# Filler stages beside lone tile stages, more gap matmuls, and longer planned landings in a planned delta-rule and MLP kernel

## The chip, the core and the metric

The kernel runs on one core of a Trainium2 chip. The metric is the device time of one execution in microseconds (us). The kernel before was timed three times: 564.54, 565.8 and 561.43 us, median 564.54. One further execution was profiled.

## What is computed

The reference is a gated delta rule (attention with a state that is corrected at every token) and a gated MLP on its output.

```python
# q, k, v: (4 batches, 8 heads, 768 tokens, 48); beta: (4, 8, 768)
k_n = k / (norm(k) + 1e-6)
for t in range(768):                       # S: (4, 8, 48, 48), from zero
    y[t] = q[t] @ S
    S = S + beta[t] * outer(k_n[t], v[t] - k_n[t] @ S)
x = y as (4, 768, 384)                     # heads side by side
h = relu(x @ w_in)                         # 384 -> 1024
u, v = h[..., :512], h[..., 512:]
v_n = (v - mean(v)) / sqrt(var(v) + 1e-6)
v_s = w_spatial @ v_n + b_spatial          # over the 768 tokens
out = (u * v_s) @ w_out                    # 512 -> 384
```

## The kernel before

**The delta rule, in chunks of 64 tokens.** Four batches of twelve chunks make 48 steps, all eight heads of a batch in one step. Four steps make a group, so there are 12 groups. For a group, K·Kᵀ (stage kk) is masked and scaled on VectorE (DVE) into `ta`. It goes to DRAM and back in another layout (`ad<-ta` L621, `la<-ad` L631, queued by SyncE, SP), and 30 dependent pairs of DVE operations (`prod` L647, `pw` L654) solve the triangular system in small blocks. The result goes through DRAM again (`wd`, then back into `ta`). Then come six stages for each step, each of them 8 or 16 small matmuls (64 x 48 and the like) on TensorE (PE) into one of four banks `pt` of PSUM: e and f finish the inverse (copied by ScalarE, ACT, L725 and L737), a makes the correction from the state (`pt<-st,kv`, then DVE `kv` L756), b applies the inverse (`pt<-kv,ta`, then DVE `us` L772), c makes the next state (`pt<-us,kv`, then DVE `st` L800), qk and d make the output (`pt<-aq,us` and `pt<-kv,st`; ACT copies it into `xs`, L845). All stage matmuls are recorded at one line, L415, of a helper. The chain from step to step is a, `kv`, b, `us`, c, `st`. Stage b of step s sets `line.cur` to s, from which due times are counted.

**Tile stages in pairs.** A stage uses two of PE's four 64 x 64 quadrants: the two on the diagonal (kind "diag") or the other two (kind "anti"). Two stages of different kinds can be issued in turns, matmul by matmul, as a pair. If only one is ready, or no second bank is free, a stage goes alone.

**The MLP.** Four steps of outputs in `xs` make a block of 256 tokens. `convert` moves the last heads to other partitions through DRAM (`xd<-xs` L869, `xs<-xd` L872), ACT rounds the block to `xh` (L888), and the rest goes to `xl` (L892). With every operand split into a high and a low part, the MLP is three matmuls for each product: `mlp_v` (L923), `mlp_u` (L989), the spatial product `mlp_g` (L1021, L1024), the output `mlp_o` (L1076). These use the whole array (kind "full"), the banks `pm`, and later `pw`, which the triangular solve uses first. The weights are loaded and split at L434 to L464. The norm of k runs ahead by groups (`knn` L537, a square root `nr` L541, DVE `t` L546 to L550).

**What sets the order.** The program is written out by a planner (class `Line`) that keeps a virtual clock for each of PE, DVE, ACT, GpSimd (POOL) and SP. Every job is a generator that yields `Op(eng, occ, lat, dep, due, kind, make)`: the engine, how long it is planned to hold the engine, how long until its result is there, when it can begin, and when it is due. `step` (L117) takes the operation that can begin earliest, and among those that begin nearly together the one due first. So a planned duration decides in which order instructions stand in each engine's queue, and the chip then executes each queue strictly in that order. A DMA is an `Op` on SP, and its planned landing time (`dma(dep, due, lat)`) decides where the operations that read it stand in the other queues.

`tensor` (L154) plans PE. `area` (L135) sums planned work of the last 3.4 us. Under `LOW` (3600) the planner prefers MLP work; under `HOT` (3050) it plans at half speed (`slow`), since PE's clock is granted in full only behind enough work. `keep_warm` (L143) fills planned gaps: as long as a gap of over 0.12 us is left and the area is under `FILL`, `idle` puts a matmul on a tile of ones (128 x 256, L1256 and L1259) into a free bank, whose result nobody reads. Below these are called gap matmuls. With four banks `pt` in `st_s` (class `Slots`, a list of free banks with the planned times from which they are free), a pair needs two of them (`line.room`).

Of the kernel before, what the change touches and what calls it, by code (L numbers as in the profile page):

```python
# [42 lines left out]
HOT = 3050  # L43
FILL = 4000

# [31 lines left out]
class Line:  # L77
# [4 lines left out]
    def __init__(self, t0):  # L82
        self.t = dict.fromkeys(("PE", "DVE", "ACT", "POOL", "SP"), t0)
        self.done = {}
        self.jobs = []
        self.mode = "full"
        self.cur = 0
        self.hist = []
        self.idle = self.room = None

# [66 lines left out]
    def tensor(self, e0, near):  # L157
# [81 lines left out]
def delta_rule_gated_mlp(  # L239
# [124 lines left out]

# [3 lines left out]
    st_s = Slots([x[:, 0:256] for x in banks])  # L368
    line.room = st_s.ready
    ob_s = Slots([sb(f"ob{i}", DM) for i in range(1)])  # L370
# [46 lines left out]
    def tiles_op(kind, dep, d, build, w):  # L417

        held = []

        def make():
            x = st_s.take()
            held.append(x)
            return build(psl(x[1], w))

        return Op("PE", 0, 1.3 * w, both(dep, st_s.ready), d, kind, make), held


    def load_w(buf, hi, lo, src, d):
        n = src.shape[1]  # L430
        st = buf[:, :n]
        if src.dtype == F32:
            t = yield dma(now, d, 6.0)
            nc.sync.dma_start(out=st, in_=src)  # L434
        else:
            raw = buf[:, 512 : 512 + 2 * n].bitcast(U32).rearrange("p (n two) -> p n two", two=2)
            t = yield dma(now, d, 6.0)
            nc.sync.dma_start(out=raw, in_=src.bitcast(U32).rearrange("p (n two) -> p n two", two=2))
# [71 lines left out]
    def norm(g):  # L510
# [68 lines left out]
    def kk(t):  # L579
# [3 lines left out]
        if t % n == 0:  # L583
# [40 lines left out]
    def load_la(g):  # L624
        d = due(4 * g - 7)
        src = ad_g[g].rearrange("j h n t -> (h n) j t")
        for blk in range(2):
            for par in range(2):
                l0, r0 = par * 64 + blk * 32, blk * 32
                t = yield dma(at(("ad", g), ("lanes", g - 2) if g > 2 else None), d, 4.2)  # L630
                nc.sync.dma_start(out=las[g % 2][l0 : l0 + 32], in_=src[:, r0 : r0 + 32, r0 : r0 + 32])  # L631
# [58 lines left out]
    def load_kv(s):  # L690
        t = yield dma(at(*((n, s - 3) for n in ("qk", "d", "a", "b", "c") if s >= 3)), due(s - 2.2), 4.5, 0.5)
        nc.sync.dma_start(out=kvs[s % 3], in_=kv_t[s])
# [171 lines left out]
    def convert(j, xs, t):  # L864
        x = xs[1].rearrange("p (u t) -> p u t", t=256)
        if j < NG2 - 2:
            xd = dram.tile([128, 256], F32, name="xd")
            t1 = yield dma(on(t), lately(0.3), 2.6)
            nc.sync.dma_start(out=xd[0:112], in_=x[0:112, 3])  # L869
            for h in range(2):  # L870
                t2 = yield dma(on(t1), lately(0.3), 2.6)
                nc.sync.dma_start(  # L872
# [307 lines left out]
    def widen(s, buf, pi):  # L1180
# [4 lines left out]
        nc.vector.transpose(out=tr.rearrange("p u t -> p (u t)"), in_=ta[:, s].rearrange("p u t -> p (u t)"))  # L1185
        t = yield Op("PE", 0.7, 1.0, both(on(t), pm_s.ready), d, "full")
        p = pm_s.take()
# [10 lines left out]
        nc.scalar.mul(out=pi[:, s], in_=pp, mul=hm)  # L1198
        t = yield Op("PE", 0.45, 0.75, on(t), d, "full")
        for u in range(NU):  # L1200
# [66 lines left out]

    line.idle = idle
    ET = mybir.EngineType
# [77 lines left out]
```

## Time and profile before

| what | value |
|---|---|
| three timed runs | 561.43, 564.54, 565.8 us |
| profiled execution, its own time | 563.41 us |
| its span in the trace | 561.7 us |
| mean granted clock of PE | 0.917 |
| busy: PE / weight loads / DVE / ACT / POOL | 500.4 / 451.8 / 355.0 / 218.9 / 142.7 us |
| DMA | 66.97 MB, 119 GB/s on the mean |
| first b stage, 28th, last | 62.8, 271.5, 483.1 us into the span |
| from the last b to the end | 78.6 us |

PE's row of busy time counts a matmul from its start to its modelled end. PEld is the load of the stationary operand, which runs beside the matmul before it. PEclk in the slices is the granted clock of PE in tenths of full speed (9 is 90% or more). In the windows view, each row is a stretch of the span, with busy time and number of instructions of each engine, the granted clock, the share of time in which DMA engines were busy, and their GB/s. In the timeline, a row is start, duration, engine, line, operation, tiles, and in brackets how long the engine was idle before it and what ended that. "issue" is time in which an engine waited for nothing that the profile shows.

### The profile page before, as it was taken

To read this page: it belongs to the slowest core of one execution; us is meant where nothing else is said; L and a number is where in the kernel's file an instruction comes from. 1 tells how busy PE (TensorE), PEld (TensorE's weight loads), DVE (VectorE), ACT (ScalarE), POOL (GpSimd) and SP (SyncE) were. 2 spreads that over 40 slices of the span, in tenths; PEclk is the share of its full clock that TensorE was granted. 3 is DMA by queue.
4 is the path that set the end of the run, shared out by engine and by line. 5 is a ranking of instruction groups with operands and counts; after the bars stand their busy time and mean duration, and the time that the engine had idled before them with its cause. 6 is when DMAs were issued, how large, how long until landed. Compare 5 with 4: busy or idle time off the path is not lost.

```text
span 561.7 us, 21394 instructions
## 1 busy us (share of the span) xinstructions
PE 500.4 (89%) x9040; PEld 451.8 (80%) x9040; DVE 355.0 (63%) x1434; ACT 218.9 (39%) x536; POOL 142.7 (25%) x212
## 2 busy tenths in 40 slices
PE   4936886987989989888989999999999999999997
PEld 4835775876777978788978789879987999898996
DVE  5899786976799978778958993258235341134210
ACT  3233433542636335423235645321256341137111
POOL 5534333653454341323213233311001000000000
PEclk8576695985989989989999999999999999999999
DMA  8687286768575738676865544461304010000001
GB/s 236 175 154 169 92 216 126 215 191 167 139 196 133 191 98 182 147 211 139 207 109 115 136 109 117 134 160 48 67 30 127 17 36 29 32 20 15 2 34 52
DMA packets 134252, 66.97 MB, mean 119 GB/s; under 512 B 105894, under 2 KB 123532, under 8 KB 134156
## 3 DMA queue, kind: packets, MB, share of 16 engines
q1 hardware_dynamic: 134156, 65.60, 47.9%
q8 instruction: 71, 1.16, 0.9%
q14 instruction: 25, 0.20, 0.1%
HBM read 50.11 MB, written 15.17 MB: 116 GB/s over the span
## 4 chain that ended last, share of the span: by engine, by line
PE 60%; DVE 16%; DMA 10%; ACT 4%; issue 4%; SPq 4%; POOL 1%; DVEq 0%; ACTq 0%
PE pt L415 20%; PE pm L1021 11%; PE pm L923 6%; PE pm L989 6%; PE pw L1021 5%; PE pm L1076 4%; PE pw L1076 3%; DVE pw L654 2%; DVE prod L647 2%; DMA knn<-in_k_nat 2%; PE pw L923 1%; DMA k<-in_kv_t 1%; DMA la<-ad 1%; SPq L631 1%; PE pw L989 1%
## 5 line engine op out<-in xcount | busy, mean ns | idle before, releaser
L654 DVE TENSOR_TENSOR pw<-pw,prod 128x96 f32<-128x96 f32 (+7 forms) x330 | 80.7, 250 | 4.6
L647 DVE TENSOR_TENSOR prod<-pw,la 128x126 f32<-128x126 f32 (+7 forms) x330 | 78.3, 242 | 7.9 <-ACT pw L641 2.9
L696 POOL TENSOR_TENSOR kv<-kv,cn 128x192 f32<-128x192 f32 x48 | 24.6, 513 | 142.8 <-DMA kv<-in_kv_t 122.8
L1021 PE MATMUL pm<-wsp_h,vh 128*128 128x256 f32 x204 | 60.2, 295 | 0.4 <-ACT vh L965 0.4
L415 PE MATMUL pt<-kv,st 48*64 48x64 f32 x768 | 55.5, 238 | 4.1 <-ACT ta L737 2.0
L1021 PE MATMUL pm<-wsp_h,vl 128*128 128x256 f32 x204 | 57.7, 283 | 0.2 <-DVE vl L969 0.2
L1021 PE MATMUL pm<-wsp_l,vh 128*128 128x256 f32 x204 | 57.7, 283 | 0.0
L415 PE MATMUL pt<-aq,us 64*64 64x64 f32 x768 | 53.4, 232 | 0.3 <-issue 0.3
L415 PEld LDWEIGHTS pt<-kv,st 48*64 48x64 f32 x768 | 44.0, 147 | 6.9 <-ACT ta L737 2.1
L415 PE MATMUL pt<-kv,ta 64*64 64x48 f32 x768 | 35.5, 231 | 10.4 <-DVE t L550 3.5
L415 PEld LDWEIGHTS pt<-aq,us 64*64 64x64 f32 x768 | 44.3, 148 | 0.4 <-issue 0.4
L415 PEld LDWEIGHTS pt<-kv,ta 64*64 64x64 f32 x768 | 29.7, 143 | 16.3 <-issue 5.8
L1038 DVE TENSOR_TENSOR tmp<-pm,ub 128x512 f32<-128x512 f32 x17 | 11.8, 691 | 48.8 <-PE pm L1024 48.8
L1057 ACT CAST gh<-tmp 128x512 fp32r<-128x512 f32 x24 | 14.8, 618 | 71.0 <-DVE tmp L1038 71.0
L415 PE MATMUL pt<-kv 48*64 48x64 f32 x768 | 35.7, 235 | 6.3 <-DVE t L546 4.7
L415 PE MATMUL pt<-k 48*64 48x64 f32 x640 | 29.4, 232 | 13.1 <-DVE nr L556 8.8
L1021 PEld LDWEIGHTS pm<-wsp_h,vh 128*128 128x128 f32 x204 | 38.8, 190 | 1.9 <-ACT vh L965 0.6
L415 PE MATMUL pt<-tn,ta 64*64 64x32 f32 x768 | 35.3, 234 | 5.2 <-DVE tn L711 3.8
L572 POOL TENSOR_TENSOR mc<-mpos,cn 128x256 f32<-128x256 f32 x46 | 28.6, 628 | 42.9 <-DVE ta L607 24.3
L1021 PEld LDWEIGHTS pm<-wsp_h,vl 128*128 128x128 f32 x204 | 39.0, 191 | 0.4 <-DVE vl L969 0.4
L1021 PEld LDWEIGHTS pm<-wsp_l,vh 128*128 128x128 f32 x204 | 39.0, 191 | 0.0
L415 PEld LDWEIGHTS pt<-tn,ta 64*64 64x64 f32 x768 | 30.7, 149 | 8.9 <-ACT wstage L442 3.8
(176 smaller groups left out, 1426.8 us busy)
## 6 DMA issues: line engine op xcount, KB each, us to landing
kv<-in_kv_t SPq DMA_DIRECT2D x48, 456.0 KB, 4.5
ad<-ta SPq DMA_DIRECT2D x24, 256.0 KB, 4.2
la<-ad SPq DMA_DIRECT2D x44, 128.0 KB, 4.4
out<-ob SPq DMA_DIRECT2D x24, 192.0 KB, 1.9
k<-in_kv_t SPq DMA_DIRECT2D x20, 224.0 KB, 3.9
knn<-in_k_nat SPq DMA_DIRECT2D x10, 384.0 KB, 5.6
wd<-w SPq DMA_DIRECT2D x22, 128.0 KB, 3.9
ta<-wd SPq DMA_DIRECT2D x44, 64.0 KB, 3.5
```

What stands on the lines that cost most here:

```text
L415: return lambda: nc.tensor.matmul(*a, **dict(dict(start=True, stop=True), **k))
L572: (nc.vector if t in (0, 2) else nc.gpsimd).tensor_tensor(out=mc, in0=mall, in1=cns[t // G][:, t % G, 1].unsqueeze(2).broadcast_to([128, N ...
L631: nc.sync.dma_start(out=las[g % 2][l0 : l0 + 32], in_=src[:, r0 : r0 + 32, r0 : r0 + 32])
L647: nc.vector.tensor_tensor(out=pr, in0=w[:, :n, j : j + 1].broadcast_to([128, n, m]), in1=la[:, j, j + 1 : 32].unsqueeze(1).broadcast_to([1 ...
L654: nc.vector.tensor_add(out=w[:, :n, j + 1 : 32], in0=w[:, :n, j + 1 : 32], in1=pr)
L696: nc.gpsimd.tensor_tensor(out=v, in0=v, in1=cns[s // G][:, s % G, 0].unsqueeze(2).broadcast_to([128, NU, HD]), op=ALU.mult)
L923: nc.tensor.matmul(p[1], a[:, kt, ts], w[:, kt, DH:], start=(n == 0), stop=(n == 3 * NK - 1))
L989: nc.tensor.matmul(pu[:, k], w[:, kt, d0 : d0 + 128], a[:, kt], start=(n == 0), stop=(n == 3 * NK - 1))
L1021: nc.tensor.matmul(pg[:, k], v[:, d0 : d0 + 128], w[:, si, ts], start=(n == 0), stop=False)
L1038: nc.vector.tensor_tensor(out=gt, in0=pg, in1=ut[:, hs], op=ALU.mult)
L1057: nc.scalar.copy(out=gh[:, hs], in_=gt)
L1076: nc.tensor.matmul(p[1][:, :DM], a[:, dd, ts], w[:, dd], start=(n == 0), stop=(n == 3 * ND - 1))
```

## The change

Four things, in the planner and in what it places:

1. **Filler stages.** A tile stage that finds no partner (`not f` in `tensor`) takes along a stage of the other kind that computes nothing of use: 8 or 16 matmuls of a constant (`mpos`) into a free bank, in turns with the real ones (`fake`). The condition `self.area(t) < FAKE` is always true with `FAKE = 99999`. A bank that got fillers is tagged with their kind, and until it is taken by a real stage of that kind it isn't given to another kind, nor to gap matmuls. `fake` gives nothing when no bank fits, and it opens a new one only if no bank has that kind's tag and two are free. `Slots` got the calls for this (`fit`, `ready_for`, `ready_both`), and a pair now needs one bank that fits "anti" and another that fits "diag".
2. **Gap matmuls up to a higher area.** `FILL` goes from 4000 to 7500; a gap matmul adds 256 for 0.107 us, so nearly every planned gap is filled.
3. **Longer planned landings.** Weights 6.0 to 9.0, `knn` 6.0 to 7.5, `k` 4.5 to 5.5, `la` 4.2 to 5.0, `kv` 4.5 to 6.0, `xd<-xs` 2.6 to 5.0, `xs<-xd` 2.6 to 3.8 us. The transfers are the same.
4. **Less weight for two small stages** of the first group in the history (150 for each us in place of 2300), so that the planner counts less area for them.

Lines behind the top of the kernel shift: L415 becomes L438, L845 and L888 become L868 and L911, L923 becomes L946, L989 becomes L1012, L1021 becomes L1044, L1076 becomes L1099, L1259 becomes L1282.

```diff
-FILL = 4000
+FILL = 7500
+FAKE = 99999
...
-        room = self.room(2)
+        room = self.room()
...
-            self.hist.append((self.t["PE"], op.occ * 2300))
+            self.hist.append((self.t["PE"], op.occ * (op.make or 2300)))
...
         lists = [o.make() for o, _ in picked]
         act_ = sum(o.lat * len(x) for (o, _), x in zip(picked, lists))
+        if not f and self.area(t) < FAKE:
+            more = self.fake("anti" if op.kind == "diag" else "diag", t, len(lists[0]))
+            if more:
+                lists.append(more)
+                act_ += 62 * len(more)
...
+            self.tag = {}
+
+        def fit(self, kind):
+            return sorted(f for f in self.free if self.tag.get(f[1], kind) == kind)
...
+        def ready_both(self):
+
+            a, d = self.fit("anti"), self.fit("diag")
+            t = [max(x[0], y[0]) for x in a for y in d if x[1] != y[1]]
+            return min(t) if t else None
 
-        def take(self):
-            f = min(self.free)
+        def take(self, kind=None):
+            f = min(self.free) if kind is None else self.fit(kind)[0]
             self.free.remove(f)
+            self.tag.pop(f[1], None)
             return f[1:]
...
-            x = st_s.take()
+            x = st_s.take(kind)
...
-            t = yield dma(now, d, 6.0)
+            t = yield dma(now, d, 9.0)
...
-            t = yield dma(at(("nr", g - 1), ("cn", g - 2)), d, 6.0, 0.5)
+            t = yield dma(at(("nr", g - 1), ("cn", g - 2)), d, 7.5, 0.5)
...
-            done["k", t] = yield dma(at(*busy), due(4 * g - 11), 4.0 if t < 2 * G else 4.5, 0.5)
+            done["k", t] = yield dma(at(*busy), due(4 * g - 11), 4.0 if t < 2 * G else 5.5, 0.5)
...
-                t = yield dma(at(("ad", g), ("lanes", g - 2) if g > 2 else None), d, 4.2)
+                t = yield dma(at(("ad", g), ("lanes", g - 2) if g > 2 else None), d, 5.0)
...
-            t1 = yield dma(on(t), lately(0.3), 2.6)
+            t1 = yield dma(on(t), lately(0.3), 5.0)
...
-                t2 = yield dma(on(t1), lately(0.3), 2.6)
+                t2 = yield dma(on(t1), lately(0.3), 3.8)
...
-        free = [f[2][:, 0:256] for k in (pm_s, st_s) for f in k.free if f[0] <= t]
+        free = [f[2][:, 0:256] for k in (pm_s, st_s) for f in k.free if f[0] <= t and f[1] not in k.tag]
...
+    def fake(kind, t, n):
+
+        fit = [f for f in st_s.fit(kind) if f[0] <= t]
+        own = [f for f in fit if f[1] in st_s.tag]
+        if not own and (kind in st_s.tag.values() or len(st_s.free) < 2):
+            return None
+        f = (own or fit or [None])[-1]
+        if f is None:
+            return None
+        st_s.tag[f[1]] = kind
+        p = psl(f[2], HD)
+        r = [
+            mm(p[rows_t(h) if kind == "diag" else rows_s(h), u], mpos[rows_t(h)], mpos[rows_t(h), 0:HD])
+            for u, h in UH
+        ]
+        return (r * 2)[:n]
```

In the whole program PE's gap matmuls go from 152 to 500 (ahead of the first b 82 to 203, from the first to the last b 54 to 238, behind it 16 to 59). There are 92 filler stages of 8 matmuls, 736 in all, where there were none. Real pairs go from 140 to 130, lone stages without a filler from 96 to 29. How the rows move is seen at three places.

PE among the first steps, before the change: gap matmuls (L1259), a lone b stage of one of the first steps (`pt<-kv,ta`), gap matmuls, and a pair of c (`pt<-us,kv`) and d (`pt<-kv,st`, `pt<-aq,us`).

```order
L415 MATMUL pt_206<-kv_168 64x64
L1259 MATMUL pm_207<-ones 128x256 x4
L415 MATMUL pt_204<-kv_167,ta_177 64x48 x8
L1259 MATMUL pm_207<-ones 128x256 x4
L415 MATMUL pt_205<-us_114,kv_167 64x48
L415 MATMUL pt_203<-kv_167,st_110 64x64
```

The same part of the program after the change: the end of a d stage, gap matmuls (now L1282), a lone a stage (`pt<-st,kv`), gap matmuls, and a lone qk stage (`pt<-kv`).

```order
L438 MATMUL pt_206<-aq_172,us_114 64x64 x2
L1282 MATMUL pm_207<-ones 128x256 x8
L438 MATMUL pt_204<-st_109,kv_168 64x48
L438 MATMUL pt_205<-mpos 64x48
L438 MATMUL pt_204<-st_109,kv_168 64x48
L438 MATMUL pt_205<-mpos 64x48
...
L1282 MATMUL pm_207<-ones 128x256 x11
L438 MATMUL pt_206<-kv_169 64x64
L438 MATMUL pt_203<-mpos 64x48
L438 MATMUL pt_206<-kv_169 64x64
```

Between the real matmuls of each lone stage there now stand fillers from `mpos`, and ahead of each stage 8 and 11 gap matmuls, where 4 stood.

PE behind the last b stage, before the change: two MLP v tiles of the last block, with gap matmuls between them.

```order
L923 MATMUL pw_210<-win_h,xh 128x512 x3
L923 MATMUL pw_210<-win_l,xh 128x512 x3
L923 MATMUL pw_210<-win_h,xl 128x512 x3
L1259 MATMUL pm_208<-ones 128x256 x4
L923 MATMUL pm_208<-win_h,xh 128x512 x3
```

After the change:

```order
L946 MATMUL pw_209<-win_l,xh 128x512 x3
L946 MATMUL pw_209<-win_h,xl 128x512 x3
L1282 MATMUL pm_208<-ones 128x256 x17
L946 MATMUL pm_208<-win_h,xh 128x512 x3
```

The MLP rows stand as they stood; 17 gap matmuls are where 4 were. Further on in the same part, three ahead of the spatial product and six ahead of the output product become 17 and 19.

ACT around the second block's `xh`, before the change:

```order
L725 ACTIVATE pi_91<-pt_205,hl 128x4x32
L537 ACTIVATE knn<-knn 128x384
L845 ACTIVATE xs<-pt_204 112x4x64
L888 CAST xh<-xs 128x768
L541 ACTIVATE nr_200<-ss_198 128x16
L737 COPY ta_179<-pt_205 128x4x32
```

After the change:

```order
L560 ACTIVATE knn<-knn 128x384
L760 COPY ta_179<-pt_204 128x4x32
L487 CAST wsp_h<-wstage 128x768
L564 ACTIVATE nr_200<-ss_198 128x16
L868 ACTIVATE xs<-pt_203 112x4x64
L911 CAST xh<-xs 128x768
```

The square root `nr` and the copy of `ta` stood behind `xh`, which waits for `xs<-xd`; now they stand ahead of it.

More of the change, by code (lines that the diff above doesn't have):

```diff
@@ L88, in __init__ @@
         self.hist = []
-        self.idle = self.room = None
+        self.idle = self.room = self.fake = None
     def at(self, *names):
@@ L368, in delta_rule_gated_mlp @@
     st_s = Slots([x[:, 0:256] for x in banks])
-    line.room = st_s.ready
+    line.room = st_s.ready_both
     ob_s = Slots([sb(f"ob{i}", DM) for i in range(1)])
@@ L421, in make @@
         def make():
-            x = st_s.take()
+            x = st_s.take(kind)
             held.append(x)
             return build(psl(x[1], w))
-        return Op("PE", 0, 1.3 * w, both(dep, st_s.ready), d, kind, make), held
+        return Op("PE", 0, 1.3 * w, both(dep, lambda: st_s.ready_for(kind)), d, kind, make), held
     def load_w(buf, hi, lo, src, d):
@@ L436, in load_w @@
             raw = buf[:, 512 : 512 + 2 * n].bitcast(U32).rearrange("p (n two) -> p n two", two=2)
-            t = yield dma(now, d, 6.0)
+            t = yield dma(now, d, 9.0)
             nc.sync.dma_start(out=raw, in_=src.bitcast(U32).rearrange("p (n two) -> p n two", two=2))
@@ L690, in load_kv @@
     def load_kv(s):
-        t = yield dma(at(*((n, s - 3) for n in ("qk", "d", "a", "b", "c") if s >= 3)), due(s - 2.2), 4.5, 0.5)
+        t = yield dma(at(*((n, s - 3) for n in ("qk", "d", "a", "b", "c") if s >= 3)), due(s - 2.2), 6.0, 0.5)
         nc.sync.dma_start(out=kvs[s % 3], in_=kv_t[s])
@@ L1185, in widen @@
         nc.vector.transpose(out=tr.rearrange("p u t -> p (u t)"), in_=ta[:, s].rearrange("p u t -> p (u t)"))
-        t = yield Op("PE", 0.7, 1.0, both(on(t), pm_s.ready), d, "full")
+        t = yield Op("PE", 0.7, 1.0, both(on(t), pm_s.ready), d, "full", 150)
         p = pm_s.take()
@@ L1198, in widen @@
         nc.scalar.mul(out=pi[:, s], in_=pp, mul=hm)
-        t = yield Op("PE", 0.45, 0.75, on(t), d, "full")
+        t = yield Op("PE", 0.45, 0.75, on(t), d, "full", 150)
         for u in range(NU):
@@ L1266, in idle @@
         return bool(free)
-    line.idle = idle
+    def fake(kind, t, n):
[13 more added lines that the diff above has]
+        return (r * 2)[:n]
+    line.idle, line.fake = idle, fake
     ET = mybir.EngineType
```

3 lines of the change are left out of this document (added).

## The prediction

> **What bounds the kernel now.** I read the page's slices first, then the seven stretches of the windows view in which the granted clock reads 0.50 (behind step 0's start-up), then the chains there.
>
> ```profile
> span 561.7 us, 21394 instructions
> ...
> PE   4936886987989989888989999999999999999997
> ...
> PEclk8576695985989989989999999999999999999999
> ```
>
> One slice is 14.04 us. From the nineteenth on the clock is granted whole and TensorE (PE) is nearly always busy: the second half is as long as PE's work. In the first half both rows have holes.
>
> ```profile
> core 0: us, PE busy (x) PEld busy (x) DVE busy (x) ACT busy (x) POOL busy (x), PEclk, DMA share, GB/s
> 48.17:65.24 17.07, 12.26 (x423) 11.18 (x425) 13.21 (x55) 9.00 (x31) 3.84 (x6) 0.50 0.51 118
> 68.65:72.07 3.42, 3.29 (x94) 3.33 (x96) 2.17 (x13) 0.84 (x3) 2.28 (x4) 0.50 0.26 71
> 85.72:99.37 13.65, 10.02 (x150) 9.00 (x151) 9.47 (x48) 5.38 (x13) 5.57 (x7) 0.50 0.67 130
> 123.27:140.33 17.06, 13.07 (x275) 11.79 (x271) 10.36 (x35) 5.59 (x17) 4.70 (x8) 0.50 0.84 195
> 164.23:171.05 6.82, 5.94 (x71) 4.54 (x70) 6.58 (x23) 2.01 (x6) 4.52 (x5) 0.50 0.84 168
> 198.36:201.77 3.41, 3.41 (x91) 3.11 (x87) 2.25 (x12) 0.89 (x4) 2.18 (x3) 0.50 0.00 0
> 246.15:249.56 3.41, 3.41 (x121) 3.41 (x112) 2.31 (x8) 1.65 (x6) 0.51 (x1) 0.50 0.55 159
> 62.80:483.10 420.30, 386.51 (x7807) 344.09 (x7808) 286.08 (x1205) 174.81 (x428) 116.58 (x146) 0.94 0.53 128
> ```
>
> PE works 51.4 us (12.26 + 3.29 + 10.02 + 13.07 + 5.94 + 3.41 + 3.41) at half clock. The last row runs from the first b stage to the last: PE is idle there for 420.30 - 386.51 = 33.8 us, so both clock and gaps are worth something, the clock more. How much of the half-clock work ends last is in the chains of the three long stretches, in the order of the rows above:
>
> ```profile
> by line: PE pt L415 46.0%; issue 21.8%; PE pm L1192 14.8%; PE pm L1203 7.5%; ACT ub L1198 3.8%; PE pm L1259 3.0%; DVE ub L1185 2.6%; DVE prod L647 1.7%; DVE pw L654 0.2%
> ...
> by line: DMA la<-ad 26.8%; SPq L631 26.0%; PE pm L923 14.7%; PE pt L415 14.5%; SPq L869 11.1%; SPq L872 6.9%; issue 3.8%; ACT win_h L464 2.9%; SPq L692 2.8%; ACT ta L737 1.3%; ACTq L641 0.3%
> ...
> by line: DMA xd<-xs 35.3%; DMA xs<-xd 18.7%; PE pt L415 18.4%; PE pm L923 14.1%; DVE t L546 10.4%; issue 6.3%; DVE us L772 2.2%; SPq L872 1.9%; DVE kv L756 1.7%; ACT nr L541 1.3%; DVE t L550 0.6%; DVE t L548 0.4%; ACT xh L888 0.2%; ACTq L44
> ```
>
> **The fillers themselves: 0.** The timeline has lone stages (two of kk, one of b) and the first rows of a pair and of the next stage:
>
> ```profile
> 269.75 1.11 PE L415 MATMUL pt<-k 48*64 48x64 f32 x32
> 270.69 0.62 PE L415 MATMUL pt<-kv,ta 64*64 64x48 f32 x16
> ...
> 101.86 0.25 PE L415 MATMUL pt<-kv,ta 64*64 64x48 f32 x1
> ...
> 102.36 0.25 PE L415 MATMUL pt<-kv 48*64 48x64 f32 x1
> ```
>
> Two lone stages take 0.94 us, 0.47 each; a pair takes 0.50. The second kind runs in quadrants that a lone stage leaves empty. That is the cover; without it 736 filler matmuls, 92 stages of eight, would cost 92 x 0.47 = 43 us.
>
> **The clock: -18.0.** Fillers and gap matmuls (500 in place of 152) give PE work in the stretches above. On the chain PE has 71.3% of 17.07, 29.2% of 13.65 and 32.5% of 17.06, so 12.2, 4.0 and 5.5 us; the four short stretches are nearly all PE, 16.1. Half of these 37.8 us is 18.9. I take one off: right behind step 0, e, c and d still stand alone, with no free bank. Ends: 25.7 (half of all 51.4) and 6.4 (half of the last three short ones, 12.8, if in the others something else ends last).
>
> The Trainium skill, page "TensorE: Matmul & The Clock Gate", Part 1, has a gate with a half-rate state, and the 0.50 agrees. It also advises to budget the ramp below 1% of a typical span; the rows do not agree, with 64.8 us of 561.7 at half clock. By 1% this term would be 5.6 and the sum 567.5.
>
> **The landings: -5.3.** The chain of waits and the timeline, at two places where an early plan bit:
>
> ```profile
> 121.45 6.03 DMA xd<-xs
> 127.87 3.19 DMA xs<-xd
> ...
> 190.82 2.48 SPq L872
> 194.28 3.45 DMA la<-ad
> ...
> 134.47 0.31 PE L415 MATMUL pt<-kv,ta 64*64 64x48 f32 x1 [3.47 <-DVE t L550]
> ...
> 197.99 0.25 PE L415 MATMUL pt<-kv,ta 64*64 64x48 f32 x1 [1.86 <-ACT ta L737]
> ...
> ACT xh L888 <- DMA xs<-xd: 11.9, 4, 3.7
> ```
>
> The plan gave xd and xs 2.6 us each; they took 6.03 and 3.19. ACT stood at the copy of xh, the small square root behind it came late, DVE with it, and PE waited 3.47. In the new order that square root stands ahead of xh. In the second place SyncE waits 2.48 for xd with la behind it; now more transfers stand between. 3.47 + 1.86 = 5.3. Ends: 0 (the wait moves to the next transfer) and all 11.9 of xh.
>
> **The tail: +4.2.** Behind the last b the order of PE's work is the same as before, only the gap matmuls are more (16, now 59):
>
> ```profile
> 505.88 0.83 ACT L888 CAST xh<-xs 128x768 fp32r<-128x768 f32 x1 [0.58 <-PE pw L923]
> ...
> 506.37 0.64 PE L1259 MATMUL pm<-ones 128*128 128x256 f32 x4
> 506.84 0.88 PE L923 MATMUL pm<-win_h,xh 128*128 128x512 f32 x3
> ...
> 515.29 0.51 PE L1259 MATMUL pm<-ones 128*128 128x256 f32 x3
> ...
> 518.01 0.39 PE L1021 MATMUL pm<-wsp_h,vh 128*128 128x256 f32 x1 [0.41 <-ACT vh L965]
> ...
> 552.45 0.88 PE L1259 MATMUL pm<-ones 128*128 128x256 f32 x6
> 553.16 0.34 PE L1076 MATMUL pm<-wout_h,gh 128*128 128x384 f32 x1
> ```
>
> Six gap matmuls take 0.71 us, 0.118 each, and real work follows at once, so the real wait is hardly longer than four, three or six of them (xh is there at 506.71). The plan waits for xh and xl, PE at first for xh alone. Now 17, 17 and 19 stand there: 13 + 14 + 13 = 40 more, 4.7 us, three others 0.4, less 0.9 for the 0.41 and some small waits behind, which they cover. Ends: 3.0 and 5.1.
>
> **The gap matmuls between first and last b: +3.0.** There are 238 in place of 54, so 184 x 0.118 = 21.7 us. The idle time, 33.8 less 5.3, holds them, and most stand ahead of a, b and c stages, whose planned waits are the real ones. Ends: 0 and 21.7.
>
> **Mode changes and lost pairs: +2.4 and +2.4.** PE goes between tiles and whole array 284 times in that part, not 230.
>
> ```profile
> 271.98 0.28 PE L415 MATMUL pt<-aq,us 64*64 64x64 f32 x4
> 272.19 0.44 PE L1076 MATMUL pm<-wout_h,gh 128*128 128x384 f32 x1
> ```
>
> Four records last 0.12 (0.47 / 4), so the change costs 272.19 - 272.10 = 0.09; 54 are 4.9. Filler banks leave fewer real pairs (130, not 140), and up to step 27 ten more stage slots, 4.7. Either may lie in waits: half of each, ends 0 and whole.
>
> **More code to load: +3.0.**
>
> ```profile
> q8 instruction: 71, 1.16, 0.9%
> ...
> PEld pt L415 <- issue: 15.1, 25, 3.6
> ```
>
> Each load is 16 KB, and PE's 18080 records make 255 for each of 71. A filler matmul is four records, a gap matmul two: 3640 more, 14 loads. PE waited 15.1 us for issue, 0.21 for each load: 3.0. Ends: 0 and 8.4 (14 of 0.6, as 15.1 / 25).
>
> The Trainium skill, page "Runtime: NRT & Kernel Launch", section Instruction fetch mechanics, has these refills as mostly hidden; the 15.1 says not here. By it the term is 0, the sum 552.1.
>
> **Sum:** -18.0 - 5.3 + 4.2 + 3.0 + 2.4 + 2.4 + 3.0 = -8.3. The profiled execution took 563.4 (span 561.7 and 1.7 around it), 1.1 below the median of 564.5: 555.1.
>
> **Rivals.** *Filled gaps leave no slack.* Any stop of PE (a code load, a late bank) used to be made up in the next gap; now gap matmuls are in the queue ahead of the real stage, and DVE and ACT wait for it. For it: the tail, where nearly all new ones cost. Against: 33.8 us of idle time. If all 21.7 cost, it is 573.8. It decides the sign once 11.3 of the 21.7 are lost, and is slower by over 1% from 16.9.
>
> *The clock was not the bound.* In the long stretches DMA and DVE end last, and only 6.4 is won: 566.7. For it: two chains with PE near 30%. Against: 71% in the first. The skill's 1% (above) would come out near it.
>
> *Waits take up everything new.* The whole 25.7, no cost for gap matmuls, changes and pairs: -25.7 - 5.3 + 4.2 + 3.0, so 539.6. Against: the queues of DMA keep part of what PE gains.
>
> *It doesn't warm.* Banks are taken where fillers are wanted, and the clock stays: 573.1. Against: half-clock stretches end early in busy parts already.
>
> **How the numbers follow.** Forecast 0.50 (own range 548 to 562; 0.42 of it over 1% faster), whole gain 0.13, clock not the bound 0.17, no slack 0.15, no warming 0.05. A measurement tells about 1% from no change here. So faster 0.55, same 0.25, slower 0.20. The likeliest is 555.1; 541 to 570 leaves out a part of the whole gain and the two slow cases.
>
> **What would show it.** Right: clock over 0.97, no half-clock stretch past 80 us; the last b near 471 (483.1 less 12.5), the tail 4 us longer; fewer waits of xh for xs; code loads 85. Wrong: half-clock stretches past 100 us; a last b no earlier; the gap matmuls ending when their stage's data are long there.

## The result, and the profile after

The changed kernel takes 583.03 us on the median of four runs (577.31 to 585.61), beside 564.36 us of the kernel before; the ratio is 1.0308 (95% interval 1.0257 to 1.0358), so it is slower by 3%. The profiled execution took 577.31 us, with a span of 575.6, 13.9 more than the span before. Throughout this part a ratio is to the kernel before on the same chip and leaves out runs over 1.5% above their kernel's fastest, so it can differ from the ratio of the medians: for silent_fill and nofake it rests on five of ten runs (the medians of all ten give 1.008 and 1.014), for early_fill on two of four (0.998).

The page's slices after the change, each now 14.39 us:

```profile
span 575.6 us, 25036 instructions
...
PE   8966898989989899998999899999999999999997
...
PEclk9977796896999999999999999999999999999999
...
q8 instruction: 85, 1.39, 1.0%
...
PE 86%; DVE 7%; issue 4%; ACT 1%; POOL 0%; DMA 0%; ACTq 0%; DVEq 0%; POOLq 0%
```

PE is busier and its clock better (0.961 on the mean, 0.917 before), and yet the span is longer. The last row is the chain of waits: PE has 86% of it, where it had 60%, and the DMA that had 10% is gone. By this chain the transfers no longer hold the kernel; PE's own queue does.

The windows view, from the first b stage to the last, then the two stretches of half clock that are left in it, then the tail:

```profile
core 0: us, PE busy (x) PEld busy (x) DVE busy (x) ACT busy (x) POOL busy (x), PEclk, DMA share, GB/s
64.15:493.35 429.20, 411.00 (x9113) 366.64 (x9112) 286.22 (x1199) 173.58 (x427) 112.37 (x141) 0.97 0.52 126
90.80:104.45 13.65, 13.52 (x210) 12.53 (x210) 10.51 (x50) 5.55 (x14) 4.77 (x6) 0.50 0.24 70
131.75:142.00 10.25, 10.25 (x185) 8.98 (x183) 5.48 (x16) 2.85 (x8) 4.88 (x5) 0.50 0.61 139
493.35:575.60 82.25, 78.44 (x619) 76.31 (x619) 19.06 (x46) 23.36 (x50) 0.00 (x0) 1.00 0.08 26
```

The middle takes 429.20 in place of 420.30, the tail 82.25 in place of 78.6, and the first b comes at 64.15 in place of 62.80: 8.9 + 3.65 + 1.35 = 13.9. PE's idle time in the middle fell from 33.8 to 18.2 (429.20 - 411.00), 15.6 less, and 23.9 us are at half clock, where 50 were. Both gains are there. PE's busy time rose by 24.5 all the same.

The same view for the gap matmuls alone, first of the kernel before, then of the changed one; the second number of a row is PE's busy time by them:

```profile
62.80:483.10 420.30, 10.62 (x55) 7.60 (x56) 0.94 0.53 128
```

```profile
64.15:493.35 429.20, 49.19 (x239) 36.54 (x240) 0.97 0.52 126
```

They hold PE for 38.6 us more, and PE's idle time fell by 15.6. By this difference some 23 us of them didn't go into idle time.

One place shows how that comes about. The timeline of PE around step 5 of the changed kernel, with the b stage that is under way, and behind it the DVE row that makes the data for the next stage:

```profile
88.91 0.22 PE L438 MATMUL pt<-kv,ta 64*64 64x48 f32 x1
90.93 0.24 PE L438 MATMUL pt<-mpos 64*64 64x48 f32 x1 [1.80 <-issue]
...
100.33 5.77 PE L1282 MATMUL pm<-ones 128*128 128x256 f32 x31
106.03 0.25 PE L438 MATMUL pt<-us,kv 64*64 64x48 f32 x1
```

```profile
103.40 0.34 DVE L795 TENSOR_TENSOR us<-pt,cs 128x192 f32<-128x192 f32 x1
```

In the middle of a b stage with fillers PE stands for 1.80 us and waits for nothing that the profile shows (issue). Right then, at 90.80, the clock falls to half for 13.65 us, up to 104.45. At 100.33 a run of 31 gap matmuls begins. The planner gives it 4.6 us (19 matmuls at 0.107, and 12 at 0.214, where it expects half clock); it takes 5.7, of which 4.1 are at half clock. The c stage behind them has its data at 103.74 and begins at 106.03, 2.3 us late. A gap that was planned for one schedule holds PE in another.

How much PE stands at issue in the whole span is in the list of waits (total, times, longest):

```profile
PE pt L438 <- issue: 18.7, 16, 2.5
...
PE pm L1012 <- issue: 1.3, 1, 1.3
PE pm L1215 <- issue: 1.1, 1, 1.1
```

That is 21.1 us in 18 waits. The same rows before:

```profile
PE pt L415 <- issue: 5.7, 6, 1.8
...
PE pm L1192 <- issue: 1.7, 1, 1.7
PE pm L1203 <- issue: 1.5, 1, 1.5
PE pm L989 <- issue: 1.3, 1, 1.3
```

These make 10.2 in nine waits, so PE stands 10.9 us longer, with 14 more code loads. The times of the code transfers in the two traces tie these waits to them: all nine before, and all but one of the 18 after, end 1.2 to 1.6 us after a 16 KB transfer of the instruction queue (q8) has landed. The 1.80 us above is one: a transfer runs from 88.23 to 89.49, and PE goes on at 90.93. The one that is not is the longest, 2.5 us up to 173.70; what it waits for stays open. The waits don't follow the number of loads alone: most loads make no wait.

### The profile page after: what moved, and what is told of

Read it like the earlier page. It is cut to its first block, busy times and chain, and to the rows that moved or that the text cites. A ratio compares the mean times of both kernels' runs of the same rounds, so it can differ in the third digit from the quotient of the medians.

```text
span 575.6 us, 25036 instructions
## 1 busy us (share of the span) xinstructions
PE 538.4 (94%) x10860; PEld 488.7 (85%) x10860; DVE 358.6 (62%) x1436; ACT 217.7 (38%) x536; POOL 139.5 (24%) x210
## 4 chain that ended last, share of the span: by engine, by line
PE 86%; DVE 7%; issue 4%; ACT 1%; POOL 0%; DMA 0%; ACTq 0%; DVEq 0%; POOLq 0%
PE pt L438 29%; PE pm L1044 12%; PE pm L1282 10%; PE pm L946 7%; PE pm L1012 7%; PE pm L1099 6%; PE pw L1044 6%; PE pw L1099 3%; PE pw L946 2%; PE pw L1012 2%; PE pm L1047 1%; DVE ub L1188 1%; DVE ub L1181 1%; DVE pw L677 1%; DVE prod L670 1%
## 5 line engine op out<-in xcount | busy, mean ns | idle before, releaser
L1282 PE MATMUL pm<-ones 128*128 128x256 f32 x494 | 84.9, 313 | 2.5 <-ACT ones L282 2.5
L670 DVE TENSOR_TENSOR prod<-pw,la 128x96 f32<-128x96 f32 (+7 forms) x330 | 78.7, 242 | 7.6 <-ACT pw L664 2.7
L1282 PEld LDWEIGHTS pm<-ones 128*128 128x128 f32 x494 | 70.1, 207 | 8.6 <-ACT ones L282 2.5
L438 PE MATMUL pt<-mpos 64*64 64x48 f32 x1472 | 59.6, 229 | 3.7 <-issue 3.7
L1044 PE MATMUL pm<-wsp_h,vh 128*128 128x256 f32 x192 | 56.4, 294 | 0.0
L438 PEld LDWEIGHTS pt<-mpos 64*64 64x64 f32 x1472 | 51.8, 142 | 5.3 <-issue 5.3
L438 PE MATMUL pt<-aq,us 64*64 64x64 f32 x768 | 50.7, 223 | 3.8 <-issue 3.8
L1044 PE MATMUL pm<-wsp_l,vh 128*128 128x256 f32 x192 | 54.2, 282 | 0.0
L1044 PE MATMUL pm<-wsp_h,vl 128*128 128x256 f32 x192 | 54.1, 282 | 0.0
L438 PE MATMUL pt<-kv,st 48*64 48x64 f32 x768 | 52.5, 228 | 1.6 <-issue 1.1
L868 ACT ACTIVATE xs<-pt 112x256 f32<-112x256 f32 x48 | 18.3, 381 | 72.1 <-PE pt L438 63.6
L438 PEld LDWEIGHTS pt<-aq,us 64*64 64x64 f32 x768 | 41.8, 138 | 3.0 <-issue 3.0
L438 PEld LDWEIGHTS pt<-kv,st 48*64 48x64 f32 x768 | 41.6, 138 | 1.7 <-DVE us L795 0.7
L1044 PEld LDWEIGHTS pm<-wsp_h,vh 128*128 128x128 f32 x192 | 36.5, 190 | 1.3
L1044 PEld LDWEIGHTS pm<-wsp_h,vl 128*128 128x128 f32 x192 | 36.6, 191 | 0.0
L1044 PEld LDWEIGHTS pm<-wsp_l,vh 128*128 128x128 f32 x192 | 36.6, 190 | 0.0
L438 PE MATMUL pt<-kv,ta 64*64 64x48 f32 x768 | 34.9, 227 | 1.6 <-issue 1.4
```

What stands on the lines that cost most here:

```text
L438: return lambda: nc.tensor.matmul(*a, **dict(dict(start=True, stop=True), **k))
L670: nc.vector.tensor_tensor(out=pr, in0=w[:, :n, j : j + 1].broadcast_to([128, n, m]), in1=la[:, j, j + 1 : 32].unsqueeze(1).broadcast_to([1 ...
L868: nc.scalar.mul(out=xt[0:112, :, qt * 64 : qt * 64 + 64], in_=psl(held[0][1], CH)[0:112], mul=-1.0)
L1044: nc.tensor.matmul(pg[:, k], v[:, d0 : d0 + 128], w[:, si, ts], start=(n == 0), stop=False)
L1282: nc.tensor.matmul(free[0].rearrange("p (n t) -> p n t", t=128), ones, ones.unsqueeze(1).broadcast_to([128, 2, 128]), start=True, stop=True,)
```

## The experiments

Theory A: the gap matmuls hold PE when the real stage's data are there. Theory B: the new order is at fault (later planned transfers, tagged banks, lost pairs). Theory C: the fillers' instructions have to be fetched, and PE stops for them. Theory N, which came up on the way: the order before is a lucky one, and any other costs about 1%.

### The same order, with less issued

These keep the planner, and so the order of every real instruction, as in the changed kernel, and only leave out or reshape work whose result nobody reads. In each, what stands ahead of the first b stage is as in the changed kernel, except that widefill's fillers are wide there too.

**silent_gap**: gap matmuls are planned, not issued.

```diff
-        if free:
+        if free and line.cur < 1:
             nc.tensor.matmul(
```

> The plan and the order are those of the changed kernel; from the first b stage on its 297 gap matmuls are planned, but not issued. Theory A (gap matmuls stand in PE's queue when the real stage's data are there): between first and last b they hold PE for 43.0 us in place of 9.4, and only 15.6 us of idle time went. Of the time ahead of stages whose data were there, about 20 us between first and last b and 3 behind it come back, less some 10 of lost clock: 13 below the changed kernel, 570 on the median, and the tail back to 79. Theory B (the new order is at fault: transfers and fillers planned so that real work comes later, pairs lost): nothing comes back, the clock falls, 583 to 595.

573.05 us, ratio 1.0156 (1.0069 to 1.0242). Ten below the changed kernel, so A has a part, and the tail is back at 78.1. But 1.6% stays without any gap matmul. That is a net sum, since the clock that they keep up went with them (0.93 in the middle, 0.97 in the changed kernel); by itself it doesn't tell whether A is all.

**silent_fill**: fillers are planned, not issued.

```diff
             if more:
-                lists.append(more)
+                if self.cur < 1:
+                    lists.append(more)
```

> Plan, order, tagged banks and gap matmuls of the changed kernel; from the first b stage on the filler matmuls (592 of 736) are planned but not issued. Theory C, now in a narrower form (the fillers' own instructions cost: PE stands at issue for their code, 18.7 us with them, 4.5 without): most of the 10 us between the changed kernel and the one without fillers comes back, 571 to 576. Theory B, in a narrower form (tagged banks, lost pairs and the order that follows from them cost): it stays at 580 to 588.

569.72 us on the median, ratio 1.0004 (0.9952 to 1.0057): by the ratio the whole loss is gone, and by the median itself (0.8% above the kernel before) three quarters of it, with all gap matmuls in place. So A can't be the cause without the fillers. Theory B in the form of tagged banks and lost pairs falls with it, since those are all still there. The windows view of this kernel, and its waits and code loads:

```profile
66.10:478.70 412.60, 402.31 (x7969) 359.70 (x7968) 284.11 (x1199) 173.67 (x427) 111.62 (x141) 0.98 0.53 131
478.70:560.90 82.20, 78.43 (x587) 76.30 (x587) 19.06 (x46) 23.38 (x50) 0.00 (x0) 1.00 0.08 26
```

```profile
PE pt L439 <- issue: 7.4, 6, 2.5
...
PE pm L1216 <- issue: 1.7, 1, 1.7
```

```profile
q8 instruction: 76, 1.25, 0.9%
```

The middle is 16.6 us shorter than in the changed kernel, and PE stands 9.1 us at issue in the span where it stood 21.1. The clock is not worse without the fillers (0.98 here, 0.97 there): beside the gap matmuls they warm nothing that can be seen. That their stops cool it is likely, not shown. The run of gap matmuls of step 5 that took 5.77 us is here at full clock:

```profile
96.60 3.96 PE L1283 MATMUL pm<-ones 128*128 128x256 f32 x31
```

**widefill**: the same filler work in the same quadrants, in a quarter of the instructions.

```diff
         r = [
-            mm(p[rows_t(h) if kind == "diag" else rows_s(h), u], mpos[rows_t(h)], mpos[rows_t(h), 0:HD])
-            for u, h in UH
+            mm(
+                p[rows_t(h) if kind == "diag" else rows_s(h)],
+                mpos[rows_t(h)],
+                mpos[rows_t(h), 0:HD].unsqueeze(1).broadcast_to([64, NU, HD]),
+            )
+            for h in range(2)
         ]
-        return (r * 2)[:n]
+        return (r * 2)[: n // 4]
...
-                act_ += 62 * len(more)
+                act_ += 62 * len(lists[0])
```

> The changed kernel with the same plan, order, banks and gap matmuls; each filler stage is issued as 2 (or 4) matmuls of 64x192 in place of 8 (or 16) of 64x48, as much work in the same quadrants with a quarter of the instructions (184 filler matmuls, not 736). Theory C (the fillers cost by the code that they need): near the one with silent fillers, 568 to 574, code loads 77 or 78, PE at issue under 10 us. If the fillers cost by the array's time or by the clock that they take: 579 to 588.

570.66 us, ratio 1.0107 (1.0067 to 1.0147), with these waits and code loads:

```profile
PE pt L438 <- issue: 8.3, 7, 2.1
...
PE pm L1226 <- issue: 0.8, 1, 0.8
```

```profile
q8 instruction: 76, 1.25, 0.9%
```

Two of the three per cent go with the number of instructions, while the array still does the filler work. That shows that the fillers cost by their instructions. That the way goes through their code, theory C, has the waits for it: 9.1 us here and in silent_fill, 21.1 in the changed kernel, nearly all of them behind a code transfer. Whether the wide fillers still cost something stays open: by the ratios it is 1.0% beside silent_fill, by the medians next to nothing (1.009 and 1.008).

**silent_both**: both edits together.

> The changed kernel's plan, order and tagged banks, from the first b stage on without issuing its gap matmuls and without its fillers. If the two costs add up: 583 less 10 (gap matmuls) less 12.5 (fillers), 560 to 562, so that the new order by itself costs nothing. If the order costs about 1% of its own (theory N): 566 to 572.

566.87 us, ratio 1.0053 (1.001 to 1.0097). The new order by itself, its landings with it, costs half a per cent, beside a kernel before that still issues its own 70 gap matmuls from the first b on. The expected adding up was wrong, and that is the finding. The last two columns are from the profiled executions: the time from the first to the last b stage, and for how long of it PE stands at issue.

| issued from the first b on | ratio to before | 95% interval | middle, us | at issue, us |
|---|---|---|---|---|
| neither | 1.0053 | 1.001 to 1.0097 | 415.8 | 11.8 |
| gap matmuls | 1.0004 | 0.9952 to 1.0057 | 412.6 | 3.8 |
| fillers | 1.0156 | 1.0069 to 1.0242 | 425.7 | 18.7 |
| both (the changed kernel) | 1.0308 | 1.0257 to 1.0358 | 429.2 | 17.1 |

Gap matmuls without fillers change little, half a per cent to the good, which their intervals don't tell from none. With fillers they cost 1.5%. Fillers cost 1.0% where the gaps are open and 3.0% where they are filled; the difference of 2.0 has, from the four intervals, some 1.2 on either side. The windows view of the middle, first with fillers alone, then with neither:

```profile
65.00:490.70 425.70, 386.53 (x8886) 346.72 (x8885) 285.67 (x1198) 173.34 (x427) 111.42 (x141) 0.93 0.52 127
```

```profile
65.10:480.90 415.80, 380.82 (x7727) 341.69 (x7726) 284.87 (x1199) 173.23 (x427) 111.40 (x141) 0.93 0.53 130
```

With open gaps PE is idle for 39.2 us (425.70 - 386.53) and 35.0; in the changed kernel 18.2 are left. That a stop is made up in an open gap and not in a filled one would fit the ratios, but the last column doesn't show it: with fillers PE stands at issue no less where the gaps are open (18.7 us) than where they are filled (17.1). The difference lies in the kernels without fillers, 11.8 and 3.8. So fillers add 6.9 us of standing with open gaps and 13.3 with filled ones, and the middle grows by 9.9 and 16.6, both times by some 3 more. Why PE stands so little with gap matmuls alone stays open.

### One part off, or one part alone

**fill4000**: the changed kernel, without the new FILL. **nofake**: without the fillers. **oldland**: without the longer landings (all seven numbers back).

```diff
-FILL = 7500
+FILL = 4000
```

> The changed kernel with FILL at 4000 again: 158 gap matmuls in place of 500, the fillers (752) and the longer landings stay. Theory A: close to the kernel before or better, 555 to 566, since what costs is gone and the fillers still keep some clock. Theory B: as slow as the changed kernel, 577 to 587. Theory C (more code to load, PE standing at issue for 43 us in all): about half way, since 684 of 1472 + 1000 new records go, 570 to 574.

579.52 us, ratio 1.0254 (1.0208 to 1.0299). Theory A as first put, by which it would be near the kernel before, is out as the whole account.

```diff
-FAKE = 99999
+FAKE = 0
```

> The changed kernel without fillers (FAKE 0), FILL at 7500 (464 gap matmuls) and the longer landings. Theory A: the loss stays, 575 to 590, since the gap matmuls are all there. Theory B, as far as fillers and their tagged banks are meant: most of the loss goes, 562 to 570. Theory C: 1472 records fewer, 570 to 575.

573.12 us, ratio 1.0093 (1.0044 to 1.0142): two of three per cent go.

> The changed kernel with the planned landings of before; 465 gap matmuls and 592 fillers. Theory A: the loss stays or grows a little, 575 to 590. Theory B, as far as the longer landings are meant: back to 560 to 568.

572.63 us, ratio 1.014 (1.0093 to 1.0188): half of the loss goes, which neither theory had.

Each part alone on the kernel before: **b_fake** (the fillers, with the tagged banks and the smaller weights), **b_fill** (FILL 7500), **b_land** (all longer landings).

> The kernel before with the fillers alone (512 filler matmuls, FILL 4000, landings of before). With the fillers at +10 by themselves (theories B and C): 572 to 578. If they cost only together with the longer landings: 562 to 568. The prediction's own price for them, nothing but a better clock, would give 550 to 558.

> The kernel before with FILL 7500 alone (463 gap matmuls). Theory A: +4 in the tail, and the matmuls run over the time at which data are there in the middle for some 15 us against a better clock: 570 to 578. If the gap matmuls lie in waits: tail +4, clock -9: 558 to 563.

> The kernel before with the longer planned landings alone. By the prediction: 5 less, 560. By the differences so far (fillers and landings together 579.5, fillers and gap matmuls 572.6): some 4 to 7 more, 569 to 572.

567.97 us, ratio 1.0054 (1.0017 to 1.0092); 570.67 us, 1.0084 (1.0049 to 1.0119); 572.61 us, 1.0148 (1.0079 to 1.0216). No part wins on its own. The three make 0.5 + 0.8 + 1.5 = 2.9%, near the 3.1 of all together; but two of the three pairs don't add up (fillers with landings 2.5, gaps with landings 0.9), so this sum is no proof.

### The landings

**b_xd**: the kernel before with the landings of `xd` and `xs` alone, the two that the prediction priced.

```diff
-            t1 = yield dma(on(t), lately(0.3), 2.6)
+            t1 = yield dma(on(t), lately(0.3), 5.0)
...
-                t2 = yield dma(on(t1), lately(0.3), 2.6)
+                t2 = yield dma(on(t1), lately(0.3), 3.8)
```

> The kernel before with the longer landings of xd and xs alone, the two of which the prediction speaks. By the prediction's term, 5.3 less: 560. By the look of all landings together (the waits of xh for xs go, 11.9 to 1.4, and PE's idle time stays, since the MLP of that block comes later): 565 to 573.

556.84 us, ratio 0.9828 (0.9782 to 0.9874): faster by 1.7%. ACT's wait for the transfer, 11.9 before, is in this kernel's list of waits:

```profile
ACT xh L888 <- DMA xs<-xd: 1.7, 2, 1.0
```

**b_rest**: the other longer landings (weights, `knn`, `k`, `la`, `kv`) alone, `xd` and `xs` as before.

> The kernel before with the other longer landings alone (weights, knn, k, la, kv; xd and xs as before). All landings together cost 7, those of xd and xs won 8.6. If the parts add up, these cost 16: 579 to 583. If an order that differs costs about 1% whatever makes it differ (theory N): 568 to 575.

575.37 us, ratio 1.0208 (1.0129 to 1.0288). The same row there:

```profile
ACT xh L888 <- DMA xs<-xd: 12.2, 5, 4.0
```

So in these two orders two of the longer landings win, and the other five lose more; what a difference between two orders is worth is in the next run.

**b_jit**: a control, the kernel before with `kv` planned at 4.6 in place of 4.5.

```diff
-        t = yield dma(at(*((n, s - 3) for n in ("qk", "d", "a", "b", "c") if s >= 3)), due(s - 2.2), 4.5, 0.5)
+        t = yield dma(at(*((n, s - 3) for n in ("qk", "d", "a", "b", "c") if s >= 3)), due(s - 2.2), 4.6, 0.5)
```

> A control: the kernel before with one planned landing (kv) at 4.6 in place of 4.5, a change of no meaning that still moves many rows of the order. Theory N (the order before is a lucky one, and any other of the same kind costs about 1%, which is what the longer landings cost): 568 to 574. If the longer landings cost by what they say: 563 to 567.

571.21 us, ratio 1.009 (1.0053 to 1.0128). A shift of 0.1 us that means nothing costs 0.9%. This is theory N, and it takes the ground from under every comparison of two orders by about 1%, b_fake and b_fill among them. It doesn't touch the four kernels of one order above, nor widefill.

**b_xd_jit**: both edits, to see whether b_xd was luck.

> The longer landings of xd and xs with the meaningless shift of kv (4.6). If the landings of xd and xs are worth 8.6 in any order: 571.2 less 8.6, 562.6, within 560 to 565. If the 556.8 was the luck of one order: 566 to 573.

562.02 us, ratio 0.9984 (0.9942 to 1.0027). Against 1.009 with the shift alone that is 1.1% less, against 1.7% without the shift. So the landings of `xd` and `xs` win in both pairs. But the same shift costs 1.6% here (0.9828 to 0.9984), as much as the landings win: two orders can't tell their gain from luck.

**after_jit**: the changed kernel with `kv` at 6.1 in place of 6.0.

> A control on the other side: the changed kernel with kv planned at 6.1 in place of 6.0. If the loss belongs to the change (fillers' code and gap matmuls): 576 to 588. If the changed kernel's order is an unlucky one: 565 to 574.

582.78 us, ratio 1.0347 (1.0285 to 1.0409). The loss holds in one other order, so the bad luck of a single order doesn't account for it.

### Versions that the runs pointed to

**early_fill**: the kernel before with FILL 7500 up to step 15. **b_xd_early**: the same with b_xd's landings. **xd_wide**: the changed kernel with FILL 4000, wide fillers, and of the longer landings only those of `xd` and `xs`.

```diff
-        while t - self.t["PE"] > 0.12 and self.area(self.t["PE"]) < FILL:
+        while t - self.t["PE"] > 0.12 and self.area(self.t["PE"]) < (FILL if self.cur < 16 else 4000):
```

> The kernel before with FILL 7500 up to step 15 and 4000 from there on (370 gap matmuls), no fillers, landings of before. If the tail's 4 and the later gap matmuls were the cost of FILL 7500, and the warmer clock ahead of them its gain: 3 to 6 below the kernel before, 559 to 562. If the order is what counts (theory N): 566 to 572.

> The longer landings of xd and xs with FILL 7500 up to step 15. If both gains are real and add up: 8.6 and 1.3 to 6 less, 551 to 556. If they are the luck of their orders: 560 to 570.

> A version made of what the runs point to: the longer landings of xd and xs alone, fillers of 64x192 (a quarter of the instructions), FILL 4000. If wide fillers are free and the landings' gain holds: 553 to 560. If fillers still cost through banks and lost pairs: 560 to 568.

564.17 us, ratio 0.9885 (0.9797 to 0.9973); 569.55 us, 1.0126 (1.0057 to 1.0195); 562.18 us, 0.9964 (0.9914 to 1.0015). Two gains put together gave a loss, so at least one of the two was its order's. The fastest version of the study is b_xd, 1.7% under the kernel before, and the shift without meaning leaves 0.2 of that.

## Why the prediction was wrong, step by step

The prediction said 555.1 us with a chance of 0.55 for faster; it was slower by 3%. No rival went further than 573.8. The step that failed first is "More code to load: +3.0", with its end of 8.4: with the order held, issuing the fillers costs 3.0% by the ratios, some 17 us, and 2.5% by the medians, some 14, both beyond that end. In the profiled executions 13.3 of the 16.6 us by which the middle is longer are PE's standing at issue.

**The fillers themselves** do cost the array nothing. At full clock a lone stage takes 0.44 us from its first record's start to its last one's in the changed kernel, a filled one 0.46 (medians over the stages with all their records): 0.02 more each, some 2 us for all 92. The two rows of lone stages and the pair beside them had that right.

**Their code** was counted right and priced wrong. The prediction said 85 loads, and there were 85. It took 0.21 us for each, a mean over 71 loads of which nine made PE wait. A filled stage of 64 records (16 of real and 16 of filler matmuls, with as many weight loads) passes in 0.46 us, so the 255 records of a load last some 1.8 us (an estimate from these two). From the start of a code transfer to PE's going on it is 2.2 to 3.0 us in the 17 waits that one precedes. That is longer, so where such stages follow one another PE can run out of code. The number of waits went from nine to 18. In the middle PE stands 17.1 us at issue with the fillers and 3.8 without them, in the same order. Of the 3.0%, two go when only the number of instructions falls (widefill). "15.1 / 25" was a price for PEld, whose wait is partly hidden; but PE's own rows, 10.2 over 71 loads, would have given 2.0 for 14 loads. What a load costs depends on where it falls, and no mean over loads says that.

**The clock: -18.0** was half right. Half-clock time in the middle fell from 50 to 23.9, not to nothing. The two stretches left begin at 90.80 and at 131.75. The first begins at the end of the 1.80 us stop shown above, the second 1.4 us behind another:

```profile
127.72 0.63 PE L438 MATMUL pt<-ta,pi 64*64 64x32 f32 x15
130.30 0.19 PE L438 MATMUL pt<-ta,pi 64*64 64x32 f32 x1 [1.96 <-issue]
```

Two other stops as long, of 2.5 us up to 173.70 and of 1.75 up to 323.35, brought no half clock, so that a stop brings it is likely, not shown.

And 6.1 of the 18.9 (half of 12.2) came from the stretch up to 65.24, most of it ahead of the first b. There the changed kernel's clock is better too (0.84 on the mean up to the first b, 0.67 before), and the first b is 1.35 us later: that part is not PE's to win. That the fillers give "PE work in the stretches above" and so warm the clock is what silent_fill speaks against, and silent_gap beside silent_both too (0.93 in the middle with fillers and without): it was the gap matmuls that did.

**The gap matmuls in the middle: +3.0** can't be told from the clock that they bring: to leave them out also takes the clock from 0.97 or 0.98 to 0.93. The net of both is 3.5 us longer in the middle with fillers (425.7 to 429.2) and 3.2 shorter without (415.8 to 412.6). But each was dearer than 0.118, and together they held PE for longer than the end of 21.7: 38.6 us more. Partly at half clock, 31 of them take 5.77 us, 0.186 each (0.128 in silent_fill). And many stand alone between two tile stages. One alone takes 0.32 from its start to the real stage's in this row and the next one:

```profile
130.42 0.39 PE L1282 MATMUL pm<-ones 128*128 128x256 f32 x1
130.74 0.25 PE L438 MATMUL pt<-kv,ta 64*64 64x48 f32 x1
```

The reason given for the low value, that "the idle time, 33.8 less 5.3, holds them", and that the planned waits ahead of the stages "are the real ones", mistook the sum for the place: that idle time lay where stops and late transfers had put it, and the planner puts gap matmuls where its plan has gaps. At step 5 the plan's gap was 4.6 us, and the real one, from 100.33 to 103.74, 3.4.

**The tail: +4.2**; it was 3.65 (82.25 - 78.60). The place is as foreseen; `xh` is there at 517.34 and the real matmul begins at 519.02:

```profile
516.50 0.84 ACT L911 CAST xh<-xs 128x768 fp32r<-128x768 f32 x1 [0.57 <-PE pw L946]
...
516.99 2.19 PE L1282 MATMUL pm<-ones 128*128 128x256 f32 x17
...
519.02 0.86 PE L946 MATMUL pm<-win_h,xh 128*128 128x512 f32 x3
```

**The landings: -5.3** had its sign borne out where it looked, and left the rest out. ACT's wait for the transfer went as foreseen (11.9 before, 1.7 in b_xd, 2.6 in the changed kernel). Those of `xd` and `xs` win 1.7% in one order and 1.1% in another, some 9.7 and 6 us of 565; since a shift without meaning moves as much, that the size is near 5.3 can be luck. The other five numbers had no term in the sum at all, and alone they cost 2.1%. Of that, 0.9 to 1.6 is what a meaningless shift costs too; the cause of the rest stays open, since in the changed kernel's own order landings and order together cost only 0.5%.

**Mode changes and lost pairs: +2.4 each.** Not tried one by one. Lost pairs are in silent_both, with the order and the landings, 0.5% or 3 us in all. The mode changes that came new lie between tile stages and gap matmuls, which silent_both doesn't issue, so no run tells their price.

**The rival** *Filled gaps leave no slack* came nearest: its 573.8 is the highest time in the prediction, the profiled execution took 577.3, and it had a chance of 0.15. That "gap matmuls are in the queue ahead of the real stage" when its data are there is shown at step 5 (2.3 us) and in the tail (1.7). That a stop "used to be made up in the next gap" and no longer is isn't shown: what the four kernels of one order show is that fillers and gap matmuls cost more together than the sum of the two alone, and with fillers PE stands at issue about as long in open gaps as in filled ones. The rival was weighed against 33.8 us of idle time, which is no argument, since by its own mechanism that idle time is the slack. And it took the stops as they were, while the change brought 10.9 us more of them.

Of the prediction's signs of being right, the tail and the 85 code loads came, and fewer waits of `xh`; the clock over 0.97, the last b near 471 and the end of half clock by 80 us didn't (0.961, 493.35, 142.00). All three signs of being wrong came.

By the rule of the Trainium skill on refills, weighed in the prediction (page "Runtime: NRT & Kernel Launch", section Instruction fetch mechanics: mostly hidden, a term of 0), the sum would have been further off still; widefill and silent_fill show that here they are not hidden.

## What to carry to other kernels

Work that fills an engine for free still has instructions: count them against the speed at which the engine passes through that stretch, and give filler work as few and as large instructions as it can have. Before filling idle time in an in-order queue, ask whether the plan's gaps lie where the chip's are, since a filler that is still running holds the real work behind it. Where a planner sets the order, time a change that means nothing (a landing moved by 0.1 us) first: here that alone is 0.4, 0.9 and 1.6% in the three kernels where it was tried, and parts are told apart below that only with the order held and the issue changed.

## What was not expected of the hardware

- PE stops for its own code in tile stages, for up to 3.0 us at a time (in silent_gap at 152.77, 1.4 us after a code transfer had landed). Its longest wait at issue there, 4.5 us, has no such transfer close ahead of it (the last had landed 4.4 us before its end), and what it waits for is open:

```profile
PE pt L438 <- issue: 21.5, 17, 4.5
```

- A stop of 1.80 us was followed at once by 13.65 us of half clock, and one of 1.96, 1.4 us later, by 10.25, in stretches that both before and behind the stop were full of work. Stops of 2.5 and 1.75 in the same execution were not.
- Matmuls of 64 x 48 in free quadrants did not keep the clock up: the granted clock is 0.961 with them and 0.970 without beside gap matmuls, and 0.931 and 0.930 without gap matmuls, all in the same order. With them PE also stops more, so what their work alone does to the clock isn't separated.
